# Attention values with the probabilities as stationary operand, and x transposed by single f16 elements

## Chip, cores, metric

One core of one Trainium2 chip. The metric is the device time of one execution in microseconds (us), median over runs. The traces come from the hardware profiler and give the span from the first to the last instruction, 1.65 to 1.87 us below the time of the same run. The granted clock is the share of full speed that the throttle gave TensorE, as the traces record it.

## The reference, cut to what matters

```python
# q, k, v: (8 batches, 8 heads, 576 positions, 64)
scores = q @ k.T / 8                       # masked to 0 <= i - j < 64
attn   = softmax(scores)
a      = attn @ v                          # (8, 8, 576, 64)
x      = a.transpose(0, 2, 1, 3).reshape(4608, 512)
out    = (relu(x @ w_gate) * (x @ w_val)) @ w_out      # d_ff = 1536, f32 out
```

## The kernel before: the parts that matter

The attention runs in 24 units of 192 queries and all 8 heads; the FFN runs in 12 tiles of 384 tokens (two units each). A small list of timed events (`W.at(time, function)`) weaves the attention's instructions into the FFN's stream. A tile has 96 matmuls `h` (x times gate and value weights), a gate on DVE (VectorE) for each of 12 slices, and 36 matmuls `op` (times `w_out`). Of the attention, `st` are the scores, `p` the probabilities after exp, `pv` the matmuls of p and v, `x` their normalized result and `xt` the same transposed, which `h` reads. The values of a unit, before:

```python
def u_pv_wide(u):                              # v stationary (with columns of ones), p moving
    for c in (0, 2, 1, 3):
        for e in range(2):
            h = 2 * c + e
            for w in range(UB):                # 3 blocks of 64 queries
                nc.tensor.matmul(d["pv"][c % 2][:, c // 2, e, 64*w:64*w + 64],
                    v16[:, w, 128*h - 64*e:128*h - 64*e + 128],        # 128 x 128 stationary
                    d["p"][h % G][:, h // G, 64*w:64*w + 64], ...)     # 64 columns moving
def u_copy(u, n): ...     # ScalarE: pv -> xv (SBUF)
def u_sum(u, half): ...   # DVE: 32x32 transposes of the row sums out of PSUM -> sT
def u_back(u): ...        # DVE: reciprocal, transpose back -> rs
def u_norm(u): ...        # DVE: xt = xv * rs            (xt is x transposed: channels on partitions)
...
def v_load(u): ...        # 3 loads of 64 keys; DVE copies give each key block its second place
```

The softmax here doesn't subtract the row's maximum and nothing guards it: scores larger than these inputs give would overflow.

## Time and profile before

| | before |
|---|---|
| time | 339.16 us (338.89 to 339.62) |
| span, granted TensorE clock (of the profiled run, which took 339.75 us) | 337.9 us, 0.994 |
| busy: TensorE (PE), DVE, ScalarE (ACT) | 325.5, 260.3, 176.7 us |
| first `h` matmul starts | 17.0 us |
| one undisturbed tile with two units | 25.95 us |

A line of the groups reads: source line, engine, operation, output<-input (sizes) xcount | busy us, mean ns of one | idle time of the engine before them and what ended it. The prediction below shows the lines that carry it. Two more lines of the groups of before turned out to be a warning that I passed over:

```profile
L350 DVE STREAM_TRANSPOSE rs<-rT 128x768 f32<-128x768 f32 x24 | 23.5, 978 | 0.8
L186 DVE STREAM_TRANSPOSE qT<-q 128x576 f32<-128x576 f32 x16 | 18.9, 1239 | 1.1 <-DMA q<-in_q_dram 1.1
```

Both are DVE transposes of f32. The first handles 768 elements in 978 ns, the second 576 in 1239. The second one writes its results 72 bytes apart, the first writes them in a row.

### The profile page before, as it was taken

The page shows a single profiled execution, that of the slowest core. Times are in us where ns is not written, and L with a number is a line of the kernel's source. Part 1 is how long each engine was busy: PE and PEld are TensorE (multiplying, and loading weights), DVE is VectorE, ACT ScalarE, POOL GpSimd, SP SyncE. Part 2 cuts the span into 40 slices and gives each one's busy share as a digit, 9 for nine tenths or more (in the row PEclk, how much of TensorE's full clock was granted, in tenths as well). Part 3 has the DMA queues.
Part 4 walks back from the last instruction along what each step waited for, and adds up shares of the span by engine and source line. Part 5 has one row for each costly group of instructions (what it writes and reads, how often), then busy time and mean ns, then how long its engine had stood idle before and what let it go on. Part 6 is the DMA issues. An engine that isn't in the chain of part 4 may idle for free.

```text
span 337.9 us, 8605 instructions
## 1 busy us (share of the span) xinstructions
PE 325.5 (96%) x3522; PEld 197.3 (58%) x3522; DVE 260.3 (77%) x493; ACT 176.7 (52%) x383; POOL 74.0 (22%) x121
## 2 busy tenths in 40 slices
PE   8699998999999999999999999999999999999995
PEld 4485485856546656655655655654655664664653
DVE  5878878998998874897989974888889874884430
ACT  4546165745636646645555564564564664653321
POOL 8724341250213221320210410150120200000000
PEclk9989999999999999999999999999999999999999
DMA  8999998496343933491242853296214402001002
GB/s 214 178 206 193 204 203 135 31 139 98 24 77 49 158 51 71 29 185 70 17 53 73 111 75 98 18 143 123 17 10 111 32 3 93 2 2 71 24 0 94
DMA packets 52886, 29.44 MB, mean 87 GB/s; under 512 B 39280, under 2 KB 44272, under 8 KB 52848
## 3 DMA queue, kind: packets, MB, share of 16 engines
q0 software_dynamic: 47088, 18.29, 47.4%
q1 hardware_dynamic: 5616, 10.55, 8.7%
q8 instruction: 27, 0.44, 0.6%
q14 instruction: 11, 0.09, 0.1%
q10 hardware_dynamic: 144, 0.07, 0.1%
HBM read 37.75 MB, written 9.44 MB: 140 GB/s over the span
## 4 chain that ended last, share of the span: by engine, by line
PE 81%; DVE 13%; issue 3%; DMA 2%; ACT 0%; DVEq 0%; ACTq 0%; POOLq 0%
PE h L419 52%; PE op L433 21%; PE pv L311 5%; PE st L249 3%; DVE sT L341 2%; DVE qT L186 2%; DMA q<-in_q_dram 2%; DVE g_sb L407 2%; DVE kT L186 1%; DVE xt L356 1%; DVE rs L350 1%; DVE p L270 1%; PE op L465 1%; DVE v L118 1%; DVE rT L348 0%
## 5 line engine op out<-in xcount | busy, mean ns | idle before, releaser
L419 PE MATMUL h<-xt,wg 128*128 128x384 f16 (+1 forms) x640 | 117.5, 313 | 1.7 <-DVE xt L356 1.7
L419 PE MATMUL h<-xt,wv 128*128 128x384 f16 (+1 forms) x640 | 116.7, 311 | 1.0 <-DVE g_sb L407 1.0
L407 DVE TENSOR_TENSOR g_sb<-r_sb,h 128x384 f16<-128x384 f32 x144 | 78.3, 550 | 48.8 <-PE h L419 47.1
L404 ACT ACTIVATE r_sb<-h 128x384 f32<-128x384 f32 x144 | 70.2, 492 | 67.0 <-PE h L419 55.3
L433 PE MATMUL op<-wo,g_sb 128*128 128x512 f16 x420 | 93.0, 379 | 0.0
L192 POOL DMA_DIRECT2D v<-in_v_dram x72 | 49.5, 696 | 181.0 <-PE pv L311 95.3
L419 PEld LDWEIGHTS <-wg 128*128 128x128 f16 x640 | 61.5, 99 | 36.5 <-DVE xt L356 1.6
L419 PEld LDWEIGHTS <-wv 128*128 128x128 f16 x640 | 59.0, 98 | 31.7 <-issue 1.3
L433 PEld LDWEIGHTS <-g_sb 128*128 128x128 f16 x420 | 40.3, 98 | 46.6
L341 DVE STREAM_TRANSPOSE sT<-pv 64x384 f32<-64x384 f32 x88 | 51.1, 580 | 9.7 <-PE pv L311 7.7
L329 ACT COPY xv<-pv 64x384 f32<-64x384 f32 x88 | 41.6, 473 | 21.5 <-DVE sT L341 8.1
L440 ACT COPY o_sb<-op 128x512 f32<-128x512 f32 x35 | 20.5, 586 | 54.6 <-PE op L433 54.6
L263 ACT ACTIVATE p<-st 128x384 f16<-128x384 f32 x92 | 39.7, 492 | 4.2 <-PE st L249 4.1
L270 DVE TENSOR_TENSOR p<-p,mask 128x384 f16<-128x384 f16 x88 | 27.5, 352 | 0.3 <-ACT p L263 0.2
L350 DVE STREAM_TRANSPOSE rs<-rT 128x768 f32<-128x768 f32 x24 | 23.5, 978 | 0.8
L356 DVE TENSOR_TENSOR xt<-xv,rs 128x768 f16<-128x768 f32 x24 | 22.8, 948 | 0.8
L311 PEld LDWEIGHTS <-v 128*128 128x128 f16 x528 | 18.6, 98 | 4.2 <-issue 0.8
L186 DVE STREAM_TRANSPOSE kT<-k 128x576 f32<-128x576 f32 (+1 forms) x18 | 19.7, 1121 | 1.4 <-ACT k L179 1.3
L311 PE MATMUL pv<-p,v 128*128 128x64 f16 x528 | 19.7, 193 | 1.1 <-DVE p L270 0.6
L186 DVE STREAM_TRANSPOSE qT<-q 128x576 f32<-128x576 f32 x16 | 18.9, 1239 | 1.1 <-DMA q<-in_q_dram 1.1
L249 PEld LDWEIGHTS <-kT 32*128 32x128 f16 x1152 | 11.0, 92 | 10.0 <-issue 9.9
L249 PE MATMUL st<-qT,kT 32*128 32x64 f16 x1152 | 13.9, 189 | 2.3 <-DVE qT L186 2.0
(47 smaller groups left out, 91.8 us busy)
## 6 DMA issues: line engine op xcount, KB each, us to landing
out_dram<-o_sb SPq DMA_DIRECT2D x35, 256.0 KB, 2.0
q<-in_q_dram POOLq DMA_DIRECT2D x16, 288.0 KB, 8.1
v<-in_v_dram POOLq DMA_DIRECT2D x72, 64.0 KB, 3.2
k<-in_k_dram POOLq DMA_DIRECT2D x14, 288.0 KB, 6.1
wg<-in_moe_w_gate_dram POOLq DMA_DIRECT2D x3, 512.0 KB, 10.1
wv<-in_moe_w_val_dram POOLq DMA_DIRECT2D x3, 512.0 KB, 11.9
wo<-in_moe_w_out_dram POOLq DMA_DIRECT2D x3, 512.0 KB, 13.7
k<-in_k_dram SPq DMA_DIRECT2D x2, 576.0 KB, 4.0
```

What stands on the lines that cost most here:

```text
L186: nc.vector.transpose(dst.rearrange("p (i j) -> p j i", i=32)[:, j0:j1], src[:, j0:j1])
L192: nc.gpsimd.dma_start(v16s[uu][64:128, w, :, 0:64], v[b, :, k0:k0 + 64].rearrange("h p d -> p h d"))
L249: nc.tensor.matmul(d["st"][hh][g][:, c:c + 64], kT[rows, hh, ks + 64 * w:ks + 64 * w + 128, dh], qT[rows, hh, ks + 64 * w:ks + 64 * w + 64 ...
L263: nc.scalar.activation(d["p"][g].rearrange("p h c -> p (h c)"), d["st"][0][g][:, 0:2 * U], ACT.Exp, scale=scale)
L270: nc.vector.tensor_tensor(p, p, mask[:, None, :].to_broadcast([128, 2 * UB, 64]), MUL)
L311: nc.tensor.matmul(d["pv"][c % 2][:, c // 2, e, 64 * w:64 * w + 64], v16[:, w, 128 * h - 64 * e:128 * h - 64 * e + 128], d["p"][h % G][:, ...
L329: nc.scalar.copy(d["xs"][rows, n::2], d["pv"][n][rows, :, e, 0:U])
L341: nc.vector.transpose(to[64 * e:64 * e + 64, half::2], d["pv"][half][64 - 64 * e:128 - 64 * e, :, e, 0:U])
L404: nc.scalar.activation(part(r_sb), part(h1), ACT.Relu)
L407: nc.vector.tensor_tensor(g_sb[:, f:f + w, c0:c1], part(r_sb), part(h2), MUL)
L419: nc.tensor.matmul(h[:, b * n:b * n + n], wt[:, c, (f + b) * 128:(f + b) * 128 + 128], xt[:, c, c0:c1], start=(c == 0), stop=(c == NC - 1))
L433: nc.tensor.matmul(op, g_sb[:, f, bass.ds(sub * 128, 128)], wo[:, f], start=(f == 0), stop=(f == NF - 1))
```

## The change

Its intent: p (32 queries) becomes stationary and v the moving operand, with a column of ones for the row sums. So the result has queries on partitions, the sum is one column beside it, and normalizing is one DVE multiply by a reciprocal per partition. x is then turned by 32x32 transposes of single f16 elements. To let every 32x32 block land in place, even and odd channels are separated as the multiply writes; the weights are loaded with their rows in the matching order. v of a batch is loaded whole; three units are made ready before the first FFN matmul, then two at a time.

```diff
+            for w in range(UB):
+                for s in range(2):
+                    for j in range(G):
+                        c = VW * (2 * w + s)                          # VW = 66
+                        nc.tensor.matmul(
+                            to[32 * j:32 * j + 32, c:c + D + 1], p_of(u, G * hh + j, w)[:, 32 * s:32 * s + 32],
+                            v16s[b % 2][:, vw, G * hh + j, 0:D + 1], start=True, stop=True, ...)
...
+    def u_norm(u, hh):
+        nc.vector.tensor_tensor(d["x"][:, hh].rearrange("p s e c -> p s c e"),
+                                pv_of(d, u, hh)[:, :, 0:D].rearrange("p s (c e) -> p s c e", e=2),
+                                d["r"][:, hh, :, :, None].to_broadcast([128, SB, D // 2, 2]), MUL)
+    def u_turn(u, hhs=(0, 1)):
+            dst = xt_tile(u // 2)[:, 2 * hh:2 * hh + 2, c0:c0 + U].rearrange("p e (s c) -> p s e c", c=32)
+            nc.vector.transpose(dst, d["x"][:, hh])
...
-            W.at(T + t, lambda g=g: u_copy(u, g))                     # xv copies, sT, rT, rs: gone
...
+        def pair(t, TA, TB, P):                                       # both pv of a tile together
+            W.at(P, lambda: u_pv(2 * t) + u_pv(2 * t + 1))
...
+        W.advance(16.8)
+        for f in range(0, NF, 4):
+            hidden(0, 0, TT, f, f + 4, 4)                             # tile 0 and half of tile 1
+            hidden(1, 0, U, f, f + 4, 4)                              # over each weight slice
```

## The prediction

> **What bounds the kernel now.** I first read the busy shares and the tenths of the page.
>
> ```profile
> PE 325.5 (96%) x3522; PEld 197.3 (58%) x3522; DVE 260.3 (77%) x493; ACT 176.7 (52%) x383; POOL 74.0 (22%) x121
> ...
> PE   8699998999999999999999999999999999999995
> ...
> DVE  5878878998998874897989974888889874884430
> ```
>
> TensorE is in use from end to end; so the time is its work in a row, plus every stretch in which it has none. DVE is high as well but should be able to hide. The groups of instructions give the size of the work:
>
> ```profile
> L419 PE MATMUL h<-xt,wv 128*128 128x384 f16 x512 | 103.5, 326 | 0.2 <-DVE g_sb L407 0.2
> L433 PE MATMUL op<-wo,g_sb 128*128 128x512 f16 x420 | 93.0, 379 | 0.0
> L341 DVE STREAM_TRANSPOSE sT<-pv 64x384 f32<-64x384 f32 x88 | 51.1, 580 | 9.7 <-PE pv L311 7.7
> L329 ACT COPY xv<-pv 64x384 f32<-64x384 f32 x88 | 41.6, 473 | 21.5 <-DVE sT L341 8.1 <-PE pv L311 7.5 <-PE h L419 5.1
> ```
>
> The mean of one matmul (326 ns) contains its latency, so I take rates from the chain that ended last (start, length, what):
>
> ```profile
> 17.00 6.93 PE h L419 x64
> ...
> 102.51 0.48 PE st L249 x39
> 102.99 4.01 PE h L419 x24
> 107.00 0.70 PE pv L311 x24
> 107.70 7.80 PE h L419 x48
> ```
>
> 7.80/48 = 0.1625 us for one h matmul (384 columns); a pv of one unit (192 queries) costs 0.70, an st 0.48. In the same chain 36 op matmuls take 7.77. A step (one tile of 384 tokens) is 96 h (15.60) + 36 op (7.77) = 23.37 us, and 12 steps are 280.4; no change to the attention touches that. Last, the table of windows, cut where the chain shows steps to begin:
>
> ```profile
> 0.00:17.00 17.00, 12.86 (x214) 7.69 (x215) 11.95 (x28) 8.65 (x22) 13.45 (x27) 0.99 1.31 196
> 17.00:44.23 27.23, 26.73 (x239) 17.51 (x239) 23.01 (x43) 11.58 (x26) 9.80 (x15) 0.94 1.42 197
> 44.23:101.86 57.63, 54.65 (x722) 37.82 (x720) 50.94 (x95) 32.33 (x70) 14.69 (x24) 1.00 0.70 99
> 101.86:127.81 25.95, 25.95 (x278) 15.04 (x277) 20.50 (x41) 14.46 (x31) 6.97 (x11) 1.00 0.60 93
> ```
>
> (Columns: length, then busy us of PE, PEld, DVE, ACT, POOL.) The last row is an undisturbed step: 25.95 - 23.37 = 2.58 us for two units, of which 2 x (0.48 + 0.70) = 2.36 is visible; the other 0.22 is about 0.1 us ahead of each st, whose first matmul starts 0.10 us after the h matmuls are through. So a unit costs 1.29 in the stream. Hence the books of the 337.9 us: first h at 17.0; work 280.4; 22 units in the stream 28.4; tail after the last matmul 3.6; together 329.4. **The remaining 8.5 us are stalls**. By the windows: 17.00 to 44.23 holds 23.37 + 1.2 of work, so 2.6 lost (the chain runs over DVE there: gates, memsets of v, masks); 44.23 to 101.86 holds 46.74 + 5 x 1.29, so 4.4 lost; two batch changes in the steady part lose about 0.7 each (the chain runs sT, kT, rs, xt, qT on DVE at 146 and 225 us).
>
> **What the Trainium skill says.** (1) "TensorE: Matmul & The Clock Gate", Part 3: matmuls in different row or column tiles of the array run concurrently, with starts some ns apart. The trace agrees for row tiles: 48 st matmuls (32*128) in 0.48 us, 10 ns each, against 29 ns each for the 24 full-array pv of 64 columns. For two column tiles there is the pv of units 0 and 1 (128*64): 10 matmuls in 0.195 us, 19.5 ns each. Four column tiles are in no trace yet. (2) "TensorEngine Tiling (Array Packing)", Key Properties: changing the tiling mode drains the array. The 0.10 us ahead of st, and none ahead of today's pv (128*128, like h), agree. (3) "VectorE: DVE Perf Modes", perf-mode tier table: a tensor_tensor with a PSUM operand runs at one element a cycle. The gate (384 elements, one operand in PSUM) takes 550 ns, the SBUF-only f16 mask 352. (4) "SBUF — State Buffer", section "SBUF: two separate sides": a GpSimd operation and some DVE operations lock each other out of a shared port. There are no GpSimd copies beside DVE work in this trace; the change adds them.
>
> **The change, part by part.**
> - *pv.* 24 matmuls of 64 columns become 48 of 65 columns, with 32 columns stationary, four column tiles in turn (the instruction lists count 528 + 72 against 1152). At the 10 ns of four row tiles: 0.48 us; the plan in the code books 0.54 with its drain. Two pv are now issued together, sharing one drain: 2 x 0.48 + 0.10 = 1.06, perhaps 0.9 if 9 ns. A pair of units costs 2 x (0.48 + 0.10) + 1.0 = 2.16 against 2.58. **Step: 25.5 us, 0.4 less.** (The plan's own spacing of steps goes from 25.805 to 25.4.)
> - *After pv.* Gone for each unit: four sT (4 x 0.58), rT 0.30, rs 0.98, xt 0.95, v copies 0.43 + 0.29 on DVE = 5.3 us; four xv copies on ACT = 1.9 us. New on DVE: one reciprocal of 12 elements (0.25, from rT), two multiplies from PSUM (gate's 0.55 each), two f16 transposes of 384 (0.58 each, from sT) = 2.5 us. DVE loses 2.8 x 22 = 60 us, so about 200 busy (60%); ACT falls to about 133. Neither is on the path in an undisturbed step, so this pays only in stalls.
> - *v.* 72 loads of 64 rows become 41, most of 128 rows, and the copies that give each key block its second place go to GpSimd (44; DVE keeps four, for units 0 and 3). Loads are issued many us ahead, so this is off the path once started. The weights are loaded with their rows in another order, in two pieces; the runs stay 2 KB, so I give that nothing.
> - *The gated part.* Three units are made before the first h; then tile 0 and half of tile 1 run over each weight slice, 23.4 us of h with no wait for attention. That should remove the 2.6 and most of the 4.4. Left: unit 3's value chain ahead of the second half of tile 1 (from pv: 0.25 + 4 x 0.56 + hand-over = 2.9 us, with some 1.7 us of TensorE work to cover it): 1.0 lost.
> - *The start, which pays for it.* The last q transpose ends at 10.9 as now (q lands late: the trace has DVE wait for it until 7.49). Then 16 exps of 192 columns at 0.25 us (four took 1.00), until 13.5; unit 0 spread, pv, reciprocal, multiply, turn to 15.1; st of unit 2 must wait for unit 1's exps to free its banks (13.6 to 14.8), with unit 1's pv queued behind it (15.2); then 2 x (0.25 + 0.55) and 2 turns of 0.55: **first h at 18.2**, not 17.0. Weights: the first slice lands at 15.3 now (GpSimd's ninth DMA after it is held until then); 50% more v ahead of it (0.2 MB at the 140 GB/s of that stretch) makes 16.7: hidden.
>
> Sum: 18.2 + tiles 0 and 1 (2 x 23.37 + 0.25 for half-width matmuls) + unit 2's pv 0.54 + unit 3 1.12 + its stall 1.0 + pair in tile 1 2.16 = 70.0. Nine steps of 25.5 = 229.5, to 299.5. Batch changes, 4 transposes of 1.24 over 5.6 us beside gates: 5.0 + 2.4 of DVE in 5.6 us, backlog 1.8 against some 1.3 us of slack in the h banks: 6 x 0.15 = 0.9. Last step 27.0 as now (310.87 to 337.9). Span 327.4; times lie 1.26 above the span (339.16 against 337.9): 328.7. I add 1.1 for hand-overs that I can't see (about 0.1 a step): **329.8 us**.
>
> **Rivals.**
> - *Column tiles don't overlap as row tiles do.* At 19.5 ns (two tiles' rate) pv is 0.94, 0.46 more x 22 = 10 us: about 340, no gain. For it: no trace of four; against: the plan's booked 0.54 looks measured (the old code's 0.49 and 0.7 match the trace).
> - *Bank waits.* st of a pair's second unit needs both double banks, so all four exps of the first, 3.0 us earlier. ACT must do 4 x 0.49 + two relus of 0.49 = 2.9 us by then: just fits. If not, 0.3 to 0.6 a step, 3 to 6 us: 333 to 336, "same".
> - *The start grows*: strided writes of the multiply, or GpSimd copies slow, by 1 to 2 us: 331 to 332.
> - *DVE's relief is worth more than I say*: all stalls go, pv at 9 ns: 326.5.
>
> **Range and chances.** Books without stalls give 326.5 to 328.5; bank waits and a late start add up to 6. Low 326.3, high 334.2. Two per cent faster is under 332.4: 0.78; same 0.20; slower needs the first rival in full: 0.02.
>
> **What would show it.** Right: first h at 18 to 19; no DVE in the chain between 20 and 42 us; a step of 25.4 to 25.6; 96 pv matmuls within 1.0 us; DVE near 200 and ACT near 133 us busy. Wrong: pv groups at over 0.6 us; h or st waiting for "ACT p" or "DVE xt" once a step; a first h after 20; DVE multiplies well over 0.55 or transposes over 0.6.

## The result

The changed kernel took **369.47 us** (366.99 to 370.74, 4 runs) against 339.39 for the kernel before in the same rounds: ratio 1.0879 (95% interval 1.0815 to 1.0943), slower. It is correct. A ratio here is the mean time of one kernel's fast runs over that of the other's fast runs of the same rounds, so not quite the ratio of the medians.

From the page of the changed kernel (busy share; tenths of 40 slices; granted TensorE clock in tenths):

```profile
PE 330.6 (91%) x4056; PEld 189.0 (52%) x4056; DVE 251.8 (69%) x397; ACT 133.0 (36%) x290; POOL 95.0 (26%) x140
...
PE   7798996969999999999989989989969969978996
...
PEclk9689999998999999999999999999989999996999
```

TensorE, busy in nearly every slice before, has holes, and some slices have a lower clock. DVE has shed only 8.5 us of its 260.3, where 60 were promised. The groups of instructions tell which of them are not as expected:

```profile
L397 PE MATMUL op<-wo,g_sb 128*128 128x512 f16 x420 | 99.0, 392 | 15.6 <-DVE g_sb L371 15.6
...
L312 DVE TENSOR_TENSOR x<-pv,r 128x384 f16<-128x384 f32 x48 | 86.9, 1967 | 0.9
...
L323 DVE STREAM_TRANSPOSE xt<-x 128x384 f16<-128x384 f16 x48 | 28.7, 635 | 0.0
```

**The multiply `x<-pv,r` takes 1967 ns; I had put 550.** The 48 of them take 86.9 us, the largest DVE group. And `op` waits 15.6 us for gates, which before it never did. The waits of TensorE in this trace (us in total, times, longest):

```profile
PE op L397 <- DVE g_sb L371: 15.6, 8, 3.7
PE h L383 <- DVE xt L323: 9.2, 5, 4.3
```

The chain that ended last shows a step (start, length, what):

```profile
208.38 0.56 PE pv L288 x40
...
208.97 0.24 DVE r L302
...
209.24 3.58 DVE x L312 x2
212.82 0.07 DVE xt L323
...
213.66 0.45 DVE g_sb L371
214.11 0.05 issue
214.16 5.57 PE op L397 x25
```

The two pv come just ahead of the last gates of the tile. In this chain the last gate stands behind two multiplies (3.58 us) and two transposes in DVE's queue, and `op`, which needs all gates, stands still. After the longest pauses of this trace (3.04, 3.73 and 4.31 us) the clock goes too: after the wait of 3.73 us at 326.9 us, the next 25 `op` took 8.13 us and not 5.57, and the windows view gives a granted clock of 0.69 from 331.0 to 338.7.

### The profile page after: what moved, and what is told of

Same layout as the page of the kernel before. It is cut to its first block, busy times and chain, and to the rows that moved or that the text cites. A ratio compares the mean times of both kernels' runs of the same rounds, so it can differ in the third digit from the quotient of the medians.

```text
span 365.3 us, 9438 instructions
## 1 busy us (share of the span) xinstructions
PE 330.6 (91%) x4056; PEld 189.0 (52%) x4056; DVE 251.8 (69%) x397; ACT 133.0 (36%) x290; POOL 95.0 (26%) x140
## 4 chain that ended last, share of the span: by engine, by line
PE 70%; DVE 24%; issue 3%; ACT 2%; DMA 1%; SPq 0%; DVEq 0%; ACTq 0%
PE h L383 49%; DVE x L312 17%; PE op L397 15%; PE st L228 3%; DVE xt L323 3%; DVE g_sb L371 2%; PE pv L288 1%; DMA k<-in_k_dram 1%; DVE r L302 1%; ACT p L262 1%; PE op L429 1%; ACT k L173 0%; DVE kT L180 0%; DVE qT L180 0%; ACT o_sb L404 0%
## 5 line engine op out<-in xcount | busy, mean ns | idle before, releaser
L397 PE MATMUL op<-wo,g_sb 128*128 128x512 f16 x420 | 99.0, 392 | 15.6 <-DVE g_sb L371 15.6
L312 DVE TENSOR_TENSOR x<-pv,r 128x384 f16<-128x384 f32 x48 | 86.9, 1967 | 0.9
L383 PEld LDWEIGHTS <-wg 128*128 128x128 f16 x624 | 58.9, 98 | 47.9 <-issue 12.2
L186 POOL DMA_DIRECT2D v<-in_v_dram x41 | 34.3, 852 | 95.6 <-PE pv L288 89.2
L262 ACT ACTIVATE p<-st 128x384 f16<-128x384 f32 (+1 forms) x104 | 41.3, 484 | 14.4 <-PE st L228 14.0
L323 DVE STREAM_TRANSPOSE xt<-x 128x384 f16<-128x384 f16 x48 | 28.7, 635 | 0.0
L195 POOL COPY v<-v 64x512 f16<-64x512 f16 (+1 forms) x22 | 15.9, 724 | 29.2 <-DMA v<-in_v_dram 28.8
L180 DVE STREAM_TRANSPOSE kT<-k 128x576 f32<-128x576 f32 x16 | 19.9, 1241 | 0.9 <-ACT k L173 0.9
L180 DVE STREAM_TRANSPOSE qT<-q 128x576 f32<-128x576 f32 x16 | 19.3, 1228 | 0.0
L197 POOL COPY v<-v 64x512 f16<-64x512 f16 (+1 forms) x22 | 16.8, 766 | 1.0
L288 PEld LDWEIGHTS <-p 128*32 128x32 f16 x1152 | 11.4, 97 | 4.6 <-issue 2.3
L288 PE MATMUL pv<-v,p 128*32 128x65 f16 x1152 | 13.2, 199 | 0.2 <-DVE p L267 0.2
```

The lines of the kernel that those rows point to most:

```text
L180: nc.vector.transpose(dst.rearrange("p (i j) -> p j i", i=32)[:, j0:j1], src[:, j0:j1])
L186: nc.gpsimd.dma_start(v16s[b % 2][lo:hi, g, :, 0:64], v[b, :, 64 * g - 64 + lo:64 * g - 64 + hi].rearrange("h p d -> p h d"))
L262: nc.scalar.activation(d["p"][i][:, UB * h0:UB * h1].rearrange("p n c -> p (n c)"), d["st"][i][:, U * h0:U * h1], ACT.Exp, scale=scale)
L288: nc.tensor.matmul(to[32 * j:32 * j + 32, c:c + D + 1], p_of(u, G * hh + j, w)[:, 32 * s:32 * s + 32], v16s[b % 2][:, vw, G * hh + j, 0:D ...
L312: nc.vector.tensor_tensor(d["x"][:, hh].rearrange("p s e c -> p s c e"), pv_of(d, u, hh)[:, :, 0:D].rearrange("p s (c e) -> p s c e", e=2) ...
L323: nc.vector.transpose(dst, d["x"][:, hh])
```

## Experiments

Theory A: the multiply is slow because of where it writes. Consecutive results (columns 2c and 2c+1) go to places 64 bytes apart. Theory B: GpSimd copies, new in this kernel, lock DVE out of a port. The Trainium skill ("SBUF — State Buffer", section "SBUF: two separate sides") says that this happens to DVE operations in a 2-port mode or with two inputs in SBUF. The multiply reads PSUM and one SBUF tile, so by the page B was unlikely from the start. Theory C: the reads, with a pitch of 66 and a broadcast operand in four dimensions. Theory D came later: the slow write harms other engines as well.

| run | what | time, us | ratio to before (95%) |
|---|---|---|---|
| e1_order | multiply writes in a row | 333.13 | 0.981 (0.978 to 0.985) |
| e2_read | natural order, transpose picks | 332.30 | 0.979 (0.976 to 0.983) |
| e3_dvespread | GpSimd copies moved to DVE | 381.16 | 1.123 (1.121 to 1.126) |
| e4_micro | DVE forms by themselves | one look | |
| e7_cost | e1 and +1.52 us a multiply | 383.53 | 1.132 (1.128 to 1.136) |
| e8_half | e1 and +0.75 us | 347.71 | 1.025 (1.022 to 1.027) |
| e9_match | e1 and +1.29 us | 371.01 | 1.094 (1.092 to 1.096) |
| e5_start | e1, start reordered | 332.56 | 0.979 (0.978 to 0.981) |
| e6_u3 | e5, unit 3 earlier | 332.66 | 0.980 (0.979 to 0.982) |
| e10_fetch | e5, fewer warming matmuls | 331.42 | 0.977 (0.975 to 0.979) |
| e11_best | e10, loads and unit 3 reordered | 330.52 | 0.975 (0.973 to 0.976) |
| e12_micro | more forms by themselves | one look | |

### e1_order: the multiply walks its elements in another order

```diff
-        nc.vector.tensor_tensor(d["x"][:, hh].rearrange("p s e c -> p s c e"),
-                                pv_of(...)[:, :, 0:D].rearrange("p s (c e) -> p s c e", e=2),
-                                d["r"][:, hh, :, :, None].to_broadcast([128, SB, D // 2, 2]), MUL)
+        nc.vector.tensor_tensor(d["x"][:, hh],
+                                pv_of(...)[:, :, 0:D].rearrange("p s (c e) -> p s e c", e=2),
+                                d["r"][:, hh, :, :, None].to_broadcast([128, SB, 2, D // 2]), MUL)
```

The same products go to the same places; only the order of the walk changes. Now PSUM is read with a step of two, and SBUF is written in a row.

> The changed kernel, but the multiply after pv walks its 384 elements so that it writes its f16 result in a row (all even columns of a 64-column block, then all odd ones) and reads PSUM with a step of two; same values, same layout. Theory A (the write pattern: neighbouring results go to addresses 64 bytes apart[...]): a multiply takes 0.55 to 0.60 us in place of 1.97, the first h comes at 17 to 18 us, no 'op' waits for g_sb, the granted clock is back at 0.99, and the time is about 330 us. Theory B (the new GpSimd copies lock DVE out of a port): still 1.97 us, time 367 to 371. Theory C (the reads: PSUM with a pitch of 66 and a broadcast reciprocal in four dimensions): still above 1.2 us, time above 345.

The page and the waits of TensorE of e1:

```profile
PE 322.5 (97%) x4056; PEld 188.3 (57%) x4056; DVE 194.5 (59%) x397; ACT 133.1 (40%) x290; POOL 95.1 (29%) x140
```
```profile
L312 DVE TENSOR_TENSOR x<-pv,r 128x384 f16<-128x384 f32 x48 | 24.9, 553 | 0.9
```
```profile
PE h L383 <- DVE xt L323: 0.3, 1, 0.3
```

The multiply takes 553 ns, no `op` waits for a gate, and the time falls by 36.3 us, from 369.47 to 333.13. B and C fall here: GpSimd's copies and the broadcast are as they were, and the reads are now the stepped ones. The books close: span 365.3 - 331.2 = 34.1 us; TensorE idle 34.7 (365.3 - 330.6) against 8.7 (331.2 - 322.5), so 26.0 us of it are waits, and for 8.1 us (330.6 - 322.5) TensorE is busy longer with the same matmuls. Most of this is the lower clock (0.967 against 0.989). A part comes from the pauses themselves: 25 `op` after a pause take 5.57 us at full clock, against 5.40 (25/36 of 7.77) without one. The time missed my mark of 330 by 3 us, and the first h came at 21.1 us, not 17 to 18; that is taken up below.

### e2_read: the other cure

```diff
+        nc.vector.tensor_tensor(d["x"][:, hh].rearrange("p s e c -> p s (e c)"), pv_of(...)[:, :, 0:D],
+                                d["r"][:, hh].to_broadcast([128, SB, D]), MUL)
...
+            src = d["x"][:, hh].rearrange("p s e c -> p s (e c)").rearrange("p s (c e) -> p s e c", e=2)
-            nc.vector.transpose(dst, d["x"][:, hh])
+            nc.vector.transpose(dst, src)
```

> The changed kernel, but the multiply writes and reads in natural order (nothing interleaved), and the f16 transpose after it picks every second element as it reads. Theory A: the multiply takes 0.55 us; reads by single f16 elements with a step of 4 bytes are free, so the transpose stays at 0.63 and the time is within 1 us of that of the first experiment; if such reads cost one cycle more an element the transpose is 1.0 us and the time some us higher. Theory B: the multiply stays at 1.97 us, time 367 to 371. Theory C: multiply 0.55 as well (all reads natural), so this run alone does not part A from C; with the first it does.

Multiply 553 ns, transpose 552 ns as in e1, 332.30 us: reading every second f16, so 4 bytes apart, costs nothing. Reads 64 bytes apart were not tried, so nothing here says whether reads pay as writes do.

### e3_dvespread: no GpSimd copies

```diff
-        act, dve, pool = nc.scalar.copy, nc.vector.tensor_copy, nc.gpsimd.tensor_copy
+        act, dve, pool = nc.scalar.copy, nc.vector.tensor_copy, nc.vector.tensor_copy
```

> The changed kernel with all copies of v's second place on DVE, none on GpSimd. Theory A: the multiply stays at 1.9 to 2.0 us, DVE gets 44 copies (some 20 us) more, time 369 to 376. Theory B: the multiply falls to 0.55 us and the time to about 335.

The multiply stayed at 1965 ns, so theory B is out. The time, 381.16 us, lies above what I gave (369 to 376): in a kernel in which DVE's queue holds up TensorE, more DVE copies cost more than I allowed (`h` waits 5.2 us for gates against 1.3 in the changed kernel, and 12.3 for xt against 9.2).

I overlooked that the traces do show GpSimd holding up another operation: the mask, which has two inputs in SBUF. In e1 one mask took 1186 ns (median 358) beside a GpSimd copy of 1.07 us, and `pv` waited 0.3 us for the masks behind it; in e3, without GpSimd copies, the longest of the 84 masks takes 361 ns. This agrees with the page named above.

### e4_micro and e12_micro: the write by itself

Both add a tail of single operations after the last output, on idle engines; `mul` and `tensor_copy` three times for each form.

```diff
+        mul(mt("m_asis", [SB, 2, D // 2]).rearrange("p s e c -> p s c e"), sce(psv), b3)
+        mul(mt("m_plain", [SB, D]), psv, rr.to_broadcast([128, SB, D]))
+        for n in (4, 8, 16):     # neighbouring results 8, 16, 32 bytes apart
+            o = mt(f"m_alt{2 * n}B", [SB, D // 2 // n, 2, n]).rearrange("p s g e c -> p (s g) c e")
...
```

> The changed kernel with a tail, after its last output, of DVE operations of 384 elements each, three of each form, on idle engines: the disputed cost by itself. Theory A: forms that write neighbouring f16 results 64 bytes apart cost 1.9 us with PSUM or SBUF sources alike, as multiply or as plain copy; the same elements written in a row cost 0.55 (0.45 from SBUF), whatever the step of the reads. Theory C: the SBUF and copy forms with the same writes are cheap. Open, and to be measured: whether f32 results 128 bytes apart, f16 results 8, 16 or 32 bytes apart, and a constant step of 4 or 64 bytes cost it too. The time itself only grows by the tail, some 40 us.

> The best kernel with another tail of single operations, to see what in the write pattern costs. If the cost comes from coming back soon to the same 4-byte word with its other half, then the alternation whose streams advance by 4 bytes (no word touched twice) is near 0.45 us for 384 elements, and the ones with 3 or 4 streams, which come back later, cost less than the 1.86 of two. If any jump of 64 bytes or more costs it, all of these are near 1.86. ScalarE's copy of the same pattern: 0.49 if only DVE is hit. A f32 transpose of 576 elements with results 72 bytes apart, as q and k have it, 1.24 us, and in a row some 0.75 us if the step is what doubles it.

DVE groups in the tail of e4 (384 elements each; mps is in PSUM, msb in SBUF):

```profile
L581 DVE TENSOR_TENSOR m_asis<-mps,mr 128x384 f16<-128x384 f32 x3 | 5.6, 1859 | 0.2
L592 DVE CAST m_copy<-mps 128x384 f16<-128x384 f32 x3 | 5.6, 1856 | 0.1
L581 DVE TENSOR_TENSOR m_sbuf<-msb,mr 128x384 f16<-128x384 f32 x3 | 5.6, 1855 | 0.1
L597 DVE CAST m_alt32B<-msb 128x384 f16<-128x384 f32 x3 | 3.3, 1096 | 0.1
L597 DVE CAST m_alt16B<-msb 128x384 f16<-128x384 f32 x3 | 3.0, 1016 | 0.1
L606 DVE CAST m_step64B<-msb 128x384 f16<-128x384 f32 x3 | 3.0, 997 | 0.1
...
L581 DVE TENSOR_TENSOR m_f<-mps,mr 128x384 f32<-128x384 f32 x3 | 2.7, 890 | 0.1
...
L581 DVE TENSOR_TENSOR m_plain<-mps,mr 128x384 f16<-128x384 f32 x3 | 1.7, 554 | 0.1
L600 DVE CAST m_ref<-msb 128x384 f16<-128x384 f32 x3 | 1.3, 429 | 0.1
L597 DVE CAST m_alt8B<-msb 128x384 f16<-128x384 f32 x3 | 1.3, 427 | 0.1
...
L603 DVE CAST m_step4B<-msb 128x384 f16<-128x384 f32 x3 | 1.1, 380 | 0.1
```

The multiply from PSUM or SBUF (m_asis, m_sbuf) and the plain copy from PSUM (m_copy) all take 1.86 us when neighbouring f16 results lie 64 bytes apart. The multiply from PSUM, written in a row, takes 554 ns. That is (1859 - 554)/384 = 3.4 ns more an element. f32 results 128 bytes apart (m_f) pay (890 - 554)/384 = 0.9 ns. Among the SBUF copies, which run faster at 429 ns for the row, 16 and 32 bytes cost it, but less: (1016 - 429)/384 = 1.5 ns an element. 8 bytes (m_alt8B) cost nothing. A constant step of 64 bytes (m_step64B, 997 ns) costs as much as the alternation does, and a constant step of 4 bytes (m_step4B, 380 ns) nothing, so going back and forth is not what costs. That fits what the Trainium skill ("SBUF — State Buffer", section "Door 1: The DMA port swizzle") says of SBUF: it has 16-byte lines, and an access that crosses to a new line pays a penalty. I had not read that as a term of my sum. The page gives no size for it; the runs do. They show the cost, and that it sets in between 8 and 16 bytes; that lines are its cause is not shown.

e12 ruled out one finer idea: streams that advance by 4 bytes, so that no word is touched twice, cost as much (1111 ns for a SBUF copy) as others do (about 1035 with streams 64 bytes apart), so it is not the return to the same word. In that run the SBUF copies with an even outer dimension are at 1.03 to 1.11 us and those with an odd one (3 blocks) at 1.9; why, no run shows. The ScalarE copies and the f32 transposes in the tail of e12:

```profile
L579 ACT CAST n_act<-mps 128x384 f16<-128x384 f32 x3 | 5.7, 1894 | 0.5 <-PE mps L202 0.4
L579 ACT CAST n_actref<-mps 128x384 f16<-128x384 f32 x3 | 1.8, 592 | 0.1
```
```profile
L579 DVE STREAM_TRANSPOSE n_tstep<-tsrc 128x576 f32<-128x576 f32 x3 | 3.8, 1259 | 0.1
...
L579 DVE STREAM_TRANSPOSE n_trow<-tsrc 128x576 f32<-128x576 f32 x3 | 2.3, 767 | 0.1
```

ScalarE pays the same (1894 against 592 ns), so moving the multiply there would not have helped. I had expected 0.49. And by these forms the transposes of q and k, which write 72 bytes apart in both kernels (1239 and 1228 to 1241 ns), pay about 0.49 us each: 1259 ns with results 72 bytes apart, 767 in a row.

### e7_cost, e8_half, e9_match: is DVE's time all of it?

```diff
+    filler = consts.tile([128, 1260], FP32, name="filler")      # 1480 in e7, 740 in e8
     def u_norm(u, hh):
...
+        nc.vector.memset(filler, 0.0)                           # after e1's fast multiply
```

> The first experiment's kernel (multiply writes in a row, 0.55 us) with a memset of 1480 columns into a spare tile after every multiply, meant to take the 1.41 us that the slow write took more. Theory A, in full: only DVE's time behind the multiply counts, so this is the changed kernel again: 366 to 372 us, op waits for g_sb some 15 us and h for xt some 9 us. Rival D: the slow write also hurts in another way (it holds a PSUM bank or SBUF's write side against TensorE or ScalarE): then this kernel is clearly faster than 366.

> The same with 740 columns, half the extra time (0.7 us a multiply, 34 us of DVE in all). If the loss is in proportion to DVE's time, about 351 us. Theory A with slack (a step loses only what its value chain exceeds the cover of the output matmuls, and gates are held by less than the banks' slack): much less than half, 334 to 342 us, hardly any throttled clock.

> The first experiment's kernel with a memset of 1260 columns behind each multiply. The earlier fillers raised the distance from one multiply to the next by 1.52 us (1480 columns, with a 0.25 us gap that I had left out) and 0.74 us (740); the slow write raises it by 1.29 (1.80 against 0.51). 1260 columns should raise it by 1.29. Theory A in full (only DVE's time counts): the time of the changed kernel, 366 to 373 us. Rival D (the slow write harms other engines too): clearly below 366.

In e7 and e8 I forgot the gap ahead of the memset. By the chain, from one multiply to the next went 2.03 us (e7) and 1.26 (e8) against 0.51 in e1 and 1.80 (3.60 for two) in the changed kernel. So e7 overshot, with 383.53 us; e9 corrects it, with 3.61 us for two:

```profile
130.51 0.56 DVE x L314
...
131.28 1.11 DVE filler L318
132.39 0.42 DVE x L314
...
133.01 1.11 DVE filler L318
134.12 0.89 DVE xt L327 x2
```
```profile
PE op L401 <- DVE g_sb L375: 16.2, 8, 3.8
PE h L387 <- DVE xt L327: 9.6, 5, 4.5
```

**e9 takes 371.01 us; the changed kernel 369.47.** Even its waits are those of the changed kernel (15.6 and 9.2). So a harmless write that takes as long on DVE does all the damage, and theory D is not needed. The response is steeper than the dose: over e1, +0.75 us a multiply costs 14.6 us, +1.29 costs 37.9, +1.52 costs 50.4. For e8 I had expected 334 to 342, as if slack would swallow most of half a dose; it took 347.71. A straight line through the first two doses starts at 0.41 us a multiply: an estimate of the slack that the queue has ahead of the last gates, less than I gave it.

### e5_start, e6_u3, e10_fetch, e11_best: the 3 us that e1 lacks, and a better version

```diff
 # e5: unit 1's values ahead of unit 2's scores
+        for hh in range(2): u_pv(1, (hh,), True); u_recip(1, (hh,)); u_norm(1, hh)
+        u_turn(1)
         u_bias(2); u_st(2); ...
-        heat(9, one_bank("heat"))
+        heat(3, one_bank("heat"))
 # e6: unit 3's scores at 43.0 in place of 45.0, batch 1's transposes at 38.8 + 1.2 i in place of 39.4 + 1.4 i
 # e10 (from e5)
-        heat(30, units[1]["st"][3][:, 384:512], False)
+        heat(8, units[1]["st"][3], False)
 # e11 (from e10): no heat(3); q and k of batch 1 loaded ahead of w_out, transposed at 31.5 + 2.0 i;
 #                 unit 3's scores at 42.2, its values at 45.0
```

> The first experiment's kernel with the start reordered: unit 1's values ahead of unit 2's scores on TensorE (they sat behind a bias group, 48 scores and a 1.2 us pause), and 3 in place of 9 warming matmuls before the first h (nine ran from 17.96 to 21.07 us at the slow clock while xt was ready at 20.2). If the missing 3 us of my books lie there, the first h comes at 18 to 19 us in place of 21.1 and the time is about 329.5 to 330.5 us. If weights or DMA bound the start instead, the first h or its wv follow-up waits for a DMA and the time stays at 332.

e5 brought the first h to 20.3 us and no more, and the time to 332.56, within the noise of e1. (The first h of e5, e10 and e11 is read in the chain, which puts it 0.1 to 0.2 us after the timeline's start; 21.1 and 22.4 are starts in the timeline.) A pause of 2.08 us had turned up in unit 1's pv, with no wait recorded. The same pause is in e1, in other work. TensorE in e1, in e5 and in e10, in order of time (start, length, what; in brackets the idle time before it):

```profile
15.03 0.56 PE L228 MATMUL st<-qT,kT 32*128 32x64 f16 x28
16.79 0.46 PE L228 MATMUL st<-qT,kT 32*128 32x64 f16 x20 [1.21 <-issue]
```
```profile
12.65 1.65 PE L288 MATMUL pv<-v,p 128*32 128x65 f16 x80
16.37 0.41 PE L288 MATMUL pv<-v,p 128*32 128x65 f16 x16 [2.08 <-issue]
```
```profile
15.43 0.23 PE L228 MATMUL st<-qT,kT 32*128 32x64 f16 x2
16.86 0.82 PE L228 MATMUL st<-qT,kT 32*128 32x64 f16 x46 [1.19 <-issue]
```

Counted from the start of the kernel, e1 has 39 warming matmuls, 12 of bias, 96 + 28 st and 48 pv before the pause; e5 has 39, 8, 96 and 80: both 223. So I took 22 warming matmuls out of e10.

> The reordered start with the 30 warming matmuls of 128 columns replaced by 8 of 512: the same array time with 22 matmuls fewer. In the reordered and in the unordered start TensorE paused with no recorded wait (1.2 and 2.1 us, ending at 16.4 to 16.8 us) after exactly the 223rd matmul. If the pause belongs to a place in the instruction stream, it comes 22 matmuls later, behind unit 1's values (in unit 2's bias or scores), unit 1's turn is done near 17.2 us and the first h comes 0.5 to 1 us earlier, at 19.3 to 19.8. If it belongs to a time or a resource, unit 1's values still stop at 14.3 and nothing changes (first h 20.3).

The pause moved behind unit 1's values, into unit 2's st, again after the 223rd matmul (17 + 12 + 96 + 96 + 2). It belongs to a place in the instruction stream, and it ends at 16.4 to 16.9 us whatever runs then. The trace shows one 16 KB packet of the instruction queue between 14 and 16 us in all three, among full data queues; a late fetch of instructions fits, but no run shows whose packet it is, so that stays open. The changed kernel (1.15 us) and e11 (0.71 us) have the pause at the same matmul. First h 19.1, time 331.42.

> As the one before, and unit 3's scores and values 2 us earlier in the plan (with batch 1's transposes ahead of it), so that its turn is done when tile 1's second half begins (it lost some 2.3 us of waiting by ScalarE's exps and the value chain from 50 to 55.5 us). Expected: 1 to 2 us less than the one before, about 328.5 us. Rival: the earlier transposes hold gates of tile 1 and cost as much as they save.

e6 gained nothing (332.66): unit 3's scores now waited 0.88 us for the batch's last q transpose, which stood behind gates and transposes on DVE at 46 to 49 us. This is close to the rival that I had named. There was also less to gain than I thought: the 2.3 us were the length of a chain over ScalarE and DVE, under which TensorE had `op` to do. TensorE itself stood still for 0.55 us there in e1 and e5 (0.24 before `pv` for a mask, 0.31 before `h` for xt).

> As e10, no warming matmuls ahead of the first h, batch 1's q and k loaded ahead of the output weights and transposed in the gated part, one every 2 us, unit 3 in the first 4 us of tile 0's output. Expected: first h at 18 to 19 us, no wait for xt at tile 1's second half (2.3 us before), steps of 25.6 as they are: 327.5 to 329.5 us by the time that the others are measured in. Rival: colder h matmuls at the start and transposes that hold gates give it back, 331 to 332.

With q and k loaded earlier and their transposes spread over the gated part, no h waits for xt. The first h starts at 17.7 us, though at the slow clock (8 matmuls in 2.67 us; granted clock 0.50 from 17.7 to 20.4 us). One loss is new: unit 3's `pv` waits 0.9 us for its masks, four of which take 2.86 us while GpSimd copies run. e11 takes **330.52 us** (330.41 to 330.88, 5 runs), ratio 0.9747 (0.9734 to 0.9760): 2.5% under the kernel before, and the fastest correct version here.

## Why the prediction was wrong

- **The step that failed** is in "After pv": "two multiplies from PSUM (gate's 0.55 each)". The duration was taken from an operation with the same sizes and types, but not with the same destination pattern. A multiply measured 1.97 us; 48 of them are 68 us more DVE time than the sum had. e1 and e2 take just this away and land at 333.1 and 332.3; e9 puts just this time back and lands at 371.0. The prediction had named the sign ("DVE multiplies well over 0.55"), and it came.
- I listed it under the rivals ("strided writes of the multiply") but sized it at 1 to 2 us, as if it lay only in the start. In truth the multiplies stand in DVE's queue ahead of each tile's last gates, so "Neither is on the path in an undisturbed step" failed with it: 8 waits of `op` (15.6 us), 5 of `h` for xt (9.2 us), and 8.1 us of longer TensorE busy time, mostly lowered clock, that no part of my text contained.
- What else the books had right, read in e1, where the multiply costs what I assumed: DVE 194.5 us (about 200), ACT 133.1 (about 133), transposes 0.55 (0.58), reciprocal 0.22 (0.25), steps of 25.57 to 25.72 (25.5) but for the first, 26.05, in which `pv` waits behind the slow mask, both pv of a pair in 0.94 us with the drain (1.06). The rival on column tiles was wrong, and the bank waits were not there (ACT ends no wait of TensorE over 0.2 us).
- The first h, put at 18.2, came at 22.4 with the slow multiplies and at 21.1 without. The rest of that miss: nine warming matmuls at the slow clock that I left out (granted clock 0.62 from 18.0 to 21.1 us in e1), unit 1's values behind unit 2's bias and scores, and the pause after the 223rd matmul. Unit 3's stall, put at 1.0, was 0.55 us of idle TensorE in e1.
- Two terms of the sum were wrong without deciding anything. "Times lie 1.26 above the span" sets the median of three runs against the span of another one; the run of that span took 339.75, so 1.85, and e1 has 1.66. And "backlog 1.8 against some 1.3 us of slack" leaves 0.5 a batch, not 0.15; e1's steps show neither.
- So without the failed term the books are still 3 us short: 329.8 us against e1's 333.1, a gain of 1.9% over the kernel before and not 2.8%. Most of the 3 us is the late first h.

## What to carry to other kernels

Take a duration only from an operation whose source and destination patterns match, not just its sizes; if a rearrangement separates neighbours, let the writes run in a row and the reads step (here by 4 bytes in SBUF or 8 in PSUM, which cost nothing). And before calling an engine's work hidden, look at what stands behind it in that engine's queue: here two slow multiplies ahead of a gate stopped TensorE while DVE was only 69% busy.

## What the Trainium skill lacked or had wrong

- "SBUF — State Buffer", section "Door 1: The DMA port swizzle": it names 16-byte lines and "a penalty", without a size. Here, for f16 results: 3.4 ns more an element 64 bytes apart in a multiply or a copy out of PSUM (1859 against 554 ns for 384 elements), 1.5 ns in most SBUF copies from 16 bytes on (1016 against 429), nothing 8 bytes apart (427). For f32 results 128 bytes apart: 0.9 ns (890 against 554). It was seen on writes; single f16 reads 4 bytes apart cost nothing (552 ns for the transpose in e1 and e2), and wider reads were not tried. Figures for 4-byte words stand on another page ("Vector Engine (DVE) Microarchitecture Reference", section "5.2 Measured stream behaviour on trn2 (trn3 not measured)"), none for f16.
- "VectorE: DVE Perf Modes", perf-mode tier table: a tensor_tensor from PSUM is given one rate. It holds for rows (553 ns); with the destination stepping it was 1859 to 1967 ns. The table has no column for the destination.
- No page that I read gives a price of a DVE transpose by its output step: 1259 ns with f32 results 72 bytes apart, 767 in a row, 576 elements each. Nor of a ScalarE copy: 1894 against 592 ns.
- No page that I read has the pause of TensorE with no wait recorded, 0.7 to 2.1 us after the 223rd matmul in five kernels (the changed one, e1, e5, e10, e11). If it is a fetch of instructions, which is not shown, it belongs to "Runtime: NRT & Kernel Launch", section "Instruction fetch mechanics".
- Nothing was wrong in "TensorE: Matmul & The Clock Gate", Part 3, which says that matmuls in different column tiles run concurrently: 96 pv matmuls in four column tiles took 0.94 us in e1, 9.8 ns each with the drain, against 29 ns for each full-array pv before.
